# First product of the last stage on pairs of token blocks by seven block products, with its weights kept in DRAM

## The chip, the cores and the metric

One Trainium2 chip, one of its cores. The metric is device time in microseconds (us) of one execution; lower is better. Matrix work runs on TensorE (PE), element work on VectorE (DVE), ScalarE (ACT) and GpSimd (POOL); DMAs are issued by SyncE (SP) unless said otherwise. Each engine, SP included, takes its instructions strictly in the order in which they stand.

## The reference

All inputs are float32 values; the six weight matrices arrive as float64 words.

```python
# attention over keys and values averaged in groups of 8 (8 batches, 8 heads, 576 tokens, 64 features)
x = attention(q, k, v)                       # [4608, 512]
a = x @ w1; b = x @ w2                       # 512 -> 1024
x = (a * b @ w3) @ w_out                     # 1024 -> 1024 -> 512
h = x @ w_in2                                # 512 -> 2048, the first product of the last stage
g = h * (1.0 / (1.0 + np.exp(-1.702 * h)))
out = g @ w_out2                             # 2048 -> 512, the second product of the last stage
```

## The kernel before

The 4608 tokens are taken in 9 blocks of 512 (`T`). Every matrix operand is held as two float32r parts, hi (rounded to 12 bits) and lo (the rest), and a product is three matmuls, hi\*hi, hi\*lo and lo\*hi (`mm3`, L93 to L97), of 128x128 weights on 512 columns. `split` (L89) makes the pair: a cast on ACT (L90) and a subtraction on DVE or POOL (L91).

There are three stages. The first multiplies w3 by w_out, with the first attention beside it. The middle one walks over the 9 blocks (L502); a step `f` of its 8 steps multiplies x by 128 columns each of w1 and w2 into the banks wk0 and wk1 (24 matmuls), ACT copies the one, DVE multiplies it by the other (L518, written to `a`), the product is split (lo on POOL), and 12 matmuls of `x2_step` take it into the four banks acc. So a step is 36 matmuls. The bank wk1 is free for the next step only when DVE's L518 is done. `tick` puts the attention of later blocks between the steps. The block's result, x2, goes to DRAM (L489).

The last stage (L575) walks over the 9 blocks again, 16 steps `f` each: 12 matmuls of w_in2 on x2 (four groups of 128 features), a sigmoid on ACT (L584), a product on DVE (L585), a split with its lo on POOL, and two steps later 12 matmuls of `out_step` into acc. A step is 24 matmuls.

The float64 weights are converted by `Conv` (L108): a chunk of 128x512 words is loaded (512 KB), ACT makes two float32 pictures of its halves (L143, L144), DVE shifts and merges (L145, L148), POOL adds (L151), and a call `done` splits the result. `conv.step` has three chunks in work at a time; a `cv` tile has four buffers. The 32 chunks of w_in2 and w_out2 are queued behind block 7 of the middle stage (L534) and are converted, two a step, beside block 8 and the first block of the last stage, into SBUF tiles (`b_s1`, `b_s2`) that stay. Tiles of 4 KB a partition come from a list of 39 slots (`take`, `give`). The order in which instructions stand on each engine is settled by a scheduler that simulates a timeline; the program's order is its starting point.

## Time and profile before

| | |
|---|---|
| runs of the kernel | 1599.31, 1599.63, 1603.57 us; median 1599.63 |
| profiled execution, span from first to last instruction | 1599.4 us (its own run time is not listed apart) |
| mean granted clock of TensorE | 0.982 of 2.4 GHz |
| matmuls | 6760 |
| read from and written to HBM | 75.5 MB and 18.9 MB |
| middle stage, blocks 7 and 8 | about 657 to 800 us |
| last stage | about 800 to 1594 us |

The page gives busy time by engine, a row of tenths over the span, the chain of work that ended last, and groups of instructions by line. A window row gives, for a stretch, the busy time of each engine with its number of instructions, the granted clock (1.00 is 2.4 GHz, 0.50 is 1.2 GHz), and the share and rate of the DMA engines. In a timeline row, the time in brackets is how long the engine sat idle before, and what it waited for. Some matmul records can be missing.

### The profile page before, as it was taken

Reading aid. Unit: us, or ns where it says so; the run is one execution under the profiler, and the core shown is the slowest. Engines: PE = TensorE matmul, PEld = TensorE weight load, DVE = VectorE, ACT = ScalarE, POOL = GpSimd, SP = SyncE. Lnnn points to the kernel's source line nnn. Section 1 sums busy time; section 2 is a strip of 40 time slices with the busy share of each in tenths; the row PEclk is TensorE's granted clock in tenths of the full one; section 3 lists DMA queues with packets and bytes.
Section 4 is the critical chain, followed back from the end, with each engine's and each line's share of the span. In section 5 each row is a group of like instructions: output and inputs, shape, how many; then the busy total and the mean of one; then the engine's idle time right before and its main releaser. Section 6 shows DMA issues by size and latency. Waiting matters only on the chain.

```text
span 1599.4 us, 19097 instructions
## 1 busy us (share of the span) xinstructions
PE 1536.5 (96%) x6920; PEld 1267.0 (79%) x6920; DVE 756.8 (47%) x1458; ACT 587.2 (37%) x1130; POOL 714.2 (45%) x748
## 2 busy tenths in 40 slices
PE   5867999999999999999998999999999999999998
PEld 3645888888888888888786888888888888888887
...
GB/s 277 244 156 58 52 72 50 78 49 72 52 72 45 75 46 34 27 80 158 146 104 27 27 27 27 20 32 20 9 40 14 33 20 33 21 27 14 27 0 27
DMA packets 195488, 95.62 MB, mean 60 GB/s; under 512 B 155457, under 2 KB 171841, under 8 KB 195393
## 3 DMA queue, kind: packets, MB, share of 16 engines
...
q8 instruction: 54, 0.88, 0.2%
...
## 4 chain that ended last, share of the span: by engine, by line
PE 82%; DVE 8%; issue 3%; DMA 2%; ACT 2%; POOL 2%; SPq 1%; DVEq 0%; POOLq 0%; ACTq 0%
PE wk L95 15%; PE wk L96 15%; PE wk L97 15%; PE acc L97 11%; PE acc L96 11%; PE acc L95 11%; DVE cv L148 2%; PE wk L246 2%; DVE cv L145 2%; DVE s L91 2%; DMA s<-in_moe_w_out_dram 1%; DVE p L281 1%; DMA s<-in_moe_w_dram 1%; POOL s L91 1%; ACT s L90 1%
## 5 line engine op out<-in xcount | busy, mean ns | idle before, releaser
L95 PE MATMUL wk<-s,s 128*128 128x512 f32 x1152 | 453.5, 395 | 7.6 <-DVE a L518 4.3
L96 PE MATMUL wk<-s,s 128*128 128x512 f32 x1152 | 451.4, 392 | 2.0 <-DVE s L358 2.0
L97 PE MATMUL wk<-s,s 128*128 128x512 f32 x1152 | 450.8, 392 | 1.4 <-DVE s L91 1.4
L91 POOL TENSOR_TENSOR s<-sg,s 128x512 fp32r<-128x512 f32 x144 | 188.6, 1310 | 508.8 <-ACT s L90 508.8
L585 DVE TENSOR_TENSOR sg<-wk,sg 128x512 f32<-128x512 f32 x144 | 99.6, 692 | 619.5 <-ACT sg L584 619.5
L97 PE MATMUL acc<-s,s 128*128 128x512 f32 x928 | 363.7, 394 | 9.5 <-DVE s L91 5.1
L95 PE MATMUL acc<-s,s 128*128 128x512 f32 x928 | 364.7, 395 | 4.3 <-ACT s L90 4.3
L96 PE MATMUL acc<-s,s 128*128 128x512 f32 x928 | 364.4, 393 | 1.6 <-DVE s L91 1.1
L95 PEld LDWEIGHTS wk<-s,s 128*128 128x128 f32 x1152 | 217.7, 189 | 54.5 <-DVE a L518 5.6
L97 PEld LDWEIGHTS wk<-s,s 128*128 128x128 f32 x1152 | 217.9, 189 | 47.5 <-DVE s L91 1.8
L96 PEld LDWEIGHTS wk<-s,s 128*128 128x128 f32 x1152 | 217.8, 189 | 46.9 <-DVE s L358 2.4
L584 ACT ACTIVATE sg<-wk 128x512 f32<-128x512 f32 x144 | 86.1, 598 | 410.9 <-PE wk L97 410.8
L97 PEld LDWEIGHTS acc<-s,s 128*128 128x128 f32 x928 | 175.6, 189 | 48.6 <-DVE s L91 8.2
L95 PEld LDWEIGHTS acc<-s,s 128*128 128x128 f32 x928 | 175.4, 189 | 41.5 <-ACT s L90 7.2
L96 PEld LDWEIGHTS acc<-s,s 128*128 128x128 f32 x928 | 175.8, 189 | 38.1 <-POOL s L91 1.8
L91 POOL TENSOR_TENSOR s<-a,s 128x512 fp32r<-128x512 f32 x72 | 94.1, 1307 | 215.8 <-ACT s L90 174.9
L281 DVE STREAM_TRANSPOSE p<-s_t 32x160 f32<-32x160 f32 (+1 forms) x560 | 178.4, 319 | 10.8
L151 POOL TENSOR_TENSOR cv<-cv,s 128x512 int32<-128x512 int32 x72 | 105.4, 1465 | 71.9 <-DVE cv L148 52.1
L90 ACT CAST s<-sg 128x512 fp32r<-128x512 f32 x144 | 89.4, 621 | 112.0 <-DVE sg L585 111.0
L518 DVE TENSOR_TENSOR a<-wk,a 128x512 f32<-128x512 f32 x72 | 49.5, 687 | 78.1 <-PE wk L97 66.4
L148 DVE SCALAR_TENSOR_TENSOR cv<-s,cv 128x512 uint32<-128x512 uint32 x72 | 80.5, 1127 | 1.0
L145 DVE TENSOR_SCALAR cv<-cv 128x512 uint32<-128x512 uint32 x72 | 61.2, 857 | 30.9 <-ACT cv L143 30.7
...
## 6 DMA issues: line engine op xcount, KB each, us to landing
s<-in_moe_w_dram SPq DMA_DIRECT2D x32, 512.0 KB, 6.8
s<-in_moe_w_out_dram SPq DMA_DIRECT2D x24, 512.0 KB, 4.6
kr<-in_k_dram SPq DMA_DIRECT2D x128, 72.0 KB, 2.4
qr<-in_q_dram SPq DMA_DIRECT2D x128, 72.0 KB, 2.5
x2d<-x2o SPq DMA_DIRECT2D x36, 256.0 KB, 2.5
x2r<-x2d SPq DMA_DIRECT2D x36, 256.0 KB, 2.9
out_dram<-o SPq DMA_DIRECT2D x36, 256.0 KB, 2.0
vr<-in_v_dram SPq DMA_DIRECT2D x32, 256.0 KB, 2.7
```

What stands on the lines that cost most here:

```text
L90: nc.scalar.copy(dst[:, 0], src)
L91: lo_eng.tensor_tensor(out=dst[:, 1], in0=src, in1=f32(dst[:, 0]), op=ALU.subtract)
L95: nc.tensor.matmul(o, a[:, 0, a_sl], b[:, 0, b_sl], start=first, stop=False)
L96: nc.tensor.matmul(o, a[:, 0, a_sl], b[:, 1, b_sl], start=False, stop=False)
L97: nc.tensor.matmul(o, a[:, 1, a_sl], b[:, 0, b_sl], start=False, stop=last)
L145: nc.vector.tensor_scalar(out=wu, in0=wu, scalar1=4, scalar2=1, op0=ALU.logical_shift_left, op1=ALU.logical_shift_right)
L148: nc.vector.scalar_tensor_tensor(out=wu, in0=hi_w, scalar=0x80000000, in1=wu, op0=ALU.bitwise_and, op1=ALU.bitwise_or)
L151: nc.gpsimd.tensor_tensor(out=w.bitcast(I32), in0=w.bitcast(I32), in1=lo_w.bitcast(I32), op=ALU.add)
L281: nc.vector.transpose(out=dst[:, :nt, 32 * c:32 * c + 32], in_=s_t[32 * c:32 * c + 32, :nt, 32 * r:32 * r + 32])
L518: nc.vector.tensor_tensor(out=a, in0=pb_, in1=a, op=ALU.mult)
L584: nc.scalar.activation(a, ps, AF.Sigmoid, scale=1.702)
L585: nc.vector.tensor_tensor(out=a, in0=ps, in1=a, op=ALU.mult)
```

## The change

**The first product of the last stage.** Blocks 1 to 8 are taken in four pairs. For a pair, the operand w_in2 is cut in two halves of its 512 inputs and two halves of its 2048 outputs, and x2 in two halves of its features and the pair's two blocks. The 2x2 block product is made with seven products instead of eight (`ORDER`: M1 to M7, each two 128-deep `mm3`, so 6 matmuls, into one of three banks), and the sums between them are made on DVE, partly while a bank is still being accumulated (`tt` after M6, `q` after M7). A step `f` of a pair stands for two output groups (f and f+8) of both blocks; it has 42 matmuls of the first product, and beside it stand 24 matmuls of the second product for the pair's first block. The second block's gated values wait in `g2`; when the 8 steps are over, they are split and multiplied in 16 `out_step`s of 12 matmuls, with `x_prep` of the next pair beside them: seven combinations of x2, each in two halves (on DVE 14 subtractions of `split` and 8 that form the combinations, from 8 loads of x2). Block 0 is taken alone as before.

**The weights.** Seven weight blocks are needed for each `f`: A11, A12, A22, and sums S1 to S4; block 0 needs A21 too. `units` and `win_second` make them from two converted chunks and write them to DRAM as hi/lo pairs (`win_d`, 2 MB for each of 8 `f`); w_out2 goes to DRAM the same way (`wout_d`). The last stage loads w_out2 once, and streams `win_d` through five buffers `st`, for block 0 and again for each pair (`pull`).

**When they are converted.** The 32 chunks are queued ahead of block 7 of the middle stage, not behind it, and all are finished before the last stage: first the 16 chunks of w_in2, then the 16 of w_out2. A pool `pc` takes the place of the attention's `pa` there and gives 9 more slots.

**The rest.** The last stage has pools of its own for SBUF and PSUM; in block 0 the conversion is gone; the output tile `o` has two buffers instead of four; the middle stage's last x2 is stored by ACT's queue. The instruction counts move thus: PE 6760 matmuls to 6568, DVE 1459 to 1797 instructions, ACT 1129 to 1205, POOL 750 to 676, SP 501 to 705.

```diff
+    win_d = [dr_p.tile([P, 8, 2, HU], F32, name=f"wind{f}", tag=f"wind{f}") for f in range(NP1)]
+    wout_d = [dr_p.tile([P, 2, T], F32, name=f"woutd{f}", tag=f"woutd{f}") for f in range(NF2)]
...
+    def resplit(t, lo_eng):
...
+        nc.scalar.copy(t[:, 0], f32(t[:, 1]))
+        lo_eng.tensor_tensor(out=t[:, 1], in0=f32(t[:, 1]), in1=f32(t[:, 0]), op=ALU.subtract)
...
+        def units(f, u0, u1, w, eng):
...
+            t = take((P, 2, 2, HU))
+            v = w.rearrange("p (u m) -> p u m", u=2)
+            nc.scalar.copy(t[:, :, 0], v)
+            eng.tensor_tensor(out=t[:, :, 1], in0=v, in1=f32(t[:, :, 0]), op=ALU.subtract)
+            nc.sync.dma_start(win_d[f][:, u0:u1 + 1], f32(t))
+            give(t)
...
+        def win_first(f):
+            def done(w):
+                hold[0] = w
+                units(f, A11, A12, w, nc.vector)
+            return done
+        def win_second(f):
+            def done(w):
+                h = hold[0]
+                a11, a12 = h[:, :HU], h[:, HU:]
+                a21, a22 = w[:, :HU], w[:, HU:]
+                units(f, A21, A22, w, nc.gpsimd)
+                c = take((P, 2, T), F32)
+                cs = c.rearrange("p a (b m) -> p (a b) m", b=2)
+                for o, p0_, p1_, op, eng in (
+                        (0, a21, a22, ALU.add, nc.vector), (2, a11, a21, ALU.subtract, nc.gpsimd),
+                        (1, cs[:, 0], a11, ALU.subtract, nc.vector),
+                        (3, a12, cs[:, 1], ALU.subtract, nc.gpsimd)):
+                    eng.tensor_tensor(out=cs[:, o], in0=p0_, in1=p1_, op=op)
+                units(f, S1, S2, c[:, 0], nc.vector)
+                units(f, S3, S4, c[:, 1], nc.gpsimd)
+                give(c)
+            return done
...
+                    (nc.scalar if blk == NB - 1 else nc.sync).dma_start(x2_d[blk][:, m], st)
...
+            if blk == NB - 2:
...
+                free[:0] = [(pa, NSLOT + i) for i in range(NX)]
+                for f in range(NP1):
+                    conv.add(col_tile(w_in2, f), None, win_first(f))
+                    conv.add(col_tile(w_in2, f + NP1), None, win_second(f))
+                for f in range(NF2):
+                    conv.add(row_tile(w_out2, f), None, wout_done(f))
+                conv.depth, conv.keep = 5, 5
+                conv.load()
...
-            if blk == NB - 2:
-                for f in range(NF2):
-                    conv.add(col_tile(w_in2, f), None, conv.to(b_s1, f))
-                    conv.add(row_tile(w_out2, f), None, conv.to(b_s2, f, nc.vector))
-                conv.load()
-            if blk < NB - 1:
-                give(*(xs.pop((blk, c)) for c in range(KM)))
+            give(*(xs.pop((blk, c)) for c in range(KM)))
...
-        rest, conv.todo = conv.todo, []
-        while any(conv.line):
-            st, conv.staged = conv.staged, []
+        while conv.busy():
             conv.step()
...
+        def pull():
...
+            if todo:
+                key, src = todo.pop(0)
+                i = st_n[0] % NST
+                st_n[0] += 1
+                t = pb.tile([P, 2, 2, HU], F32R, name="st", tag=f"st{i}")
+                nc.sync.dma_start(f32(t[:, :src.shape[1]]), src)
+                ready[key] = t
...
+        def mm3u(o, w, j, b, first, last):
+            m = sl(j)
+            for n, (x, y) in enumerate(((0, 0), (0, 1), (1, 0))):
+                nc.tensor.matmul(o, w[:, x, m], b[:, y], start=first and n == 0,
+                                 stop=last and n == 2, skip_group_check=True)
...
+        ORDER = (("M1", A11, 0, True), ("M6", S2, 1, True), ("M5", S1, 2, True), ("M7", S3, 1, False),
+                 ("M2", A12, 0, False), ("M4", A22, 1, False), ("M3", S4, 2, False))
+        HS = {A11: (0, 0), A12: (0, 1), S1: (1, 0), S2: (1, 1), S3: (2, 0), S4: (2, 1), A22: (3, 0)}
...
+        def x_prep(pr):
...
+            def load(jj):
+                for n, (c, b) in enumerate(((jj, b0), (jj, b0 + 1), (2 + jj, b0), (2 + jj, b0 + 1))):
+                    raw[jj, n] = tmp(("m1", "m1", "tt", "q")[n], 2 if n < 2 else 1)
+                    nc.sync.dma_start(raw[jj, n], x2_d[b][:, c])
...
+        for _ in range(3):
+            pull()
...
+        for c in range(KM):
+            t = gtile(c, F32R)
+            nc.sync.dma_start(f32(t[:, 1]), x2_d[0][:, c])
+            resplit(t, nc.vector if c % 2 else nc.gpsimd)
+            x.append(t)
...
+        for f in range(NF2):
+            bk = bank()
+            w = ready.pop(("h", 0, f, 0))
+            for c in range(KM):
+                mm3u(bk[1], w[:, c // 2], c % 2, x[c], c == 0, c == KM - 1)
+            pull()
...
+            if len(pend) > 2:
+                out_step(outs)
+            if f >= 4:
+                prep.pop(0)()
...
+        for pr in range(1, NPAIR + 1):
+            X = xc.pop(pr)
+            outs = [bank() for _ in range(4)]
+            g2 = []
+            for f in range(NP1):
...
+                ga, gb = moving(), moving()
+                g2.append(gtile(f))
+                c12, c22 = g2[f][:, 0], g2[f][:, 1]
...
+                def gate(v, eng):
+                    sg = tmp("sg", 2)
+                    nc.scalar.activation(sg, v, AF.Sigmoid, scale=1.702)
+                    eng.tensor_tensor(out=v, in0=v, in1=sg, op=ALU.mult)
+                for name, u, b, first in ORDER:
+                    o = B[b][1]
+                    s, h = HS[u]
+                    w = ready["h", pr, f, s]
+                    for j in range(2):
+                        mm3u(o, w[:, h], j, X[name, j], first and j == 0, j == 1)
+                    if name == "M1":
+                        m1 = tmp("m1", 2)
+                        nc.scalar.copy(m1, o)
+                    elif name == "M6":
+                        tt = tmp("tt", 1)
+                        nc.vector.tensor_tensor(out=tt, in0=o, in1=m1, op=ALU.add)
+                    elif name == "M7":
+                        q_ = tmp("q", 1)
+                        nc.vector.tensor_tensor(out=q_, in0=o, in1=m1, op=ALU.add)
+                        nc.vector.tensor_tensor(out=c22, in0=B[2][1], in1=q_, op=ALU.add)
+                        gate(c22, nc.gpsimd)
+                        pull()
+                    elif name == "M2":
+                        sg = tmp("sg", 2)
+                        nc.scalar.activation(sg, o, AF.Sigmoid, scale=1.702)
+                        nc.vector.tensor_tensor(out=sg, in0=o, in1=sg, op=ALU.mult)
+                        freed(B[0])
+                        split(ga, sg, nc.vector)
+                        pull()
+                    elif name == "M4":
+                        c21 = tmp("o", 2)
+                        nc.vector.tensor_tensor(out=c21, in0=o, in1=m1, op=ALU.add)
+                        freed(B[1])
+                        gate(c21, nc.vector)
+                        split(gb, c21, nc.vector)
+                        pull()
+                    elif name == "M3":
+                        nc.vector.tensor_tensor(out=c12, in0=o, in1=tt, op=ALU.add)
+                        freed(B[2])
+                        gate(c12, nc.gpsimd)
+                        pull()
...
+                while pend:
+                    out_step(outs)
+                pend.append((f, ga, f == 0, False))
+                pend.append((f + NP1, gb, False, f == NP1 - 1))
...
+            prep = x_prep(pr + 1) if pr < NPAIR else []
+            order = [(f, h) for f in range(NP1) for h in range(2)]
+            n, outs2 = 0, None
+            while pend:
+                while n < NF2 and len(pend) < NMV:
+                    f, h = order[n]
+                    g = moving()
+                    split(g, g2[f][:, h], nc.vector)
+                    pend.append((f + h * NP1, g, n == 0, n == NF2 - 1))
+                    n += 1
+                if prep:
+                    prep.pop(0)()
+                if pend[0][2]:
+                    store(outs, 2 * pr - 1)
+                    outs2 = [bank() for _ in range(4)]
+                out_step(outs2 or outs)
```

Three places show how the instructions stand. The names: `cv` is a chunk in conversion, `a` the middle stage's product, `s` a slot, `m_`, `tt`, `q`, `o`, `sg` single float32 tiles, `g_` the second block's gated values, `mv` a split operand of the second product, `bk_` a bank, `xM_` a split combination of x2, `wind_` and `woutd_` the weights in DRAM.

First, DVE in the middle stage, between two products `a`. Before, in block 8, where chunks of w_in2 and w_out2 take turns:

```order
L518 TENSOR_TENSOR a<-wk_68,a 128x512 [waits PE_49]
L145 TENSOR_SCALAR cv<-cv 128x512 [waits Activation_49]
L148 SCALAR_TENSOR_TENSOR cv<-s_6693,cv 128x512 [waits DMAHW2_49,DVE_49]
L91 TENSOR_TENSOR s_6973<-cv,s_6973 128x512 [waits Activation_49]
L145 TENSOR_SCALAR cv<-cv 128x512 [waits Activation_49]
L148 SCALAR_TENSOR_TENSOR cv<-s_6769,cv 128x512 [waits DVE_49]
L145 TENSOR_SCALAR cv<-cv 128x512 [waits Activation_49]
L518 TENSOR_TENSOR a<-wk_68,a 128x512 [waits PE_49]
```

Now, in block 7, where the chunks of w_in2 are made:

```order
L574 TENSOR_TENSOR a<-wk_68,a 128x512 [waits PE_49]
L420 TENSOR_TENSOR s_6782<-cv,s_6782 128x2x256 [waits Activation_49]
L156 TENSOR_SCALAR cv<-cv 128x512 [waits Activation_49,Pool_49]
L444 TENSOR_TENSOR s_6840<-cv 128x256 [waits Pool_49]
L159 SCALAR_TENSOR_TENSOR cv<-s_6628,cv 128x512 [waits DVE_49]
L444 TENSOR_TENSOR s_6840<-s_6840,cv 128x256 [waits DVE_49]
L420 TENSOR_TENSOR s_6845<-s_6840,s_6845 128x2x256 [waits DMAHW4_49,Activation_49]
L420 TENSOR_TENSOR s_6861<-cv,s_6861 128x2x256 [waits Activation_49]
L444 TENSOR_TENSOR s_6919<-cv 128x256 [waits Pool_49]
L574 TENSOR_TENSOR a<-wk_68,a 128x512 [waits PE_49,Activation_49]
```

Between two products there stood six conversion instructions, and now eight: the subtractions of `units` (L420) and the sums of weight blocks (L444, 256 columns) have come in.

Second, PE and DVE in a pair's first product. Before, a step's 12 matmuls of the first product waited for one bank and DVE made one product a step (L585). PE now, from the end of M7 of one `f` (bank bk_8709) over the second product and M1 of the next `f` to M4, which goes on in M7's bank:

```order
L644 MATMUL bk_8709<-xM_8145,st 128x512 x3
L108 MATMUL bk_8199<-wo_7931,mv 128x512
L106 MATMUL bk_8200<-wo_7931,mv 128x512
L107 MATMUL bk_8200<-wo_7931,mv 128x512
L108 MATMUL bk_8200<-wo_7931,mv 128x512
L106 MATMUL bk_8201<-wo_7931,mv 128x512
L107 MATMUL bk_8201<-wo_7931,mv 128x512
L108 MATMUL bk_8201<-wo_7931,mv 128x512
L644 MATMUL bk_8814<-xM_7758,st 128x512 [waits DMAHW3_49]
L644 MATMUL bk_8814<-xM_7758,st 128x512 x2
L644 MATMUL bk_8814<-xM_8071,st 128x512 x3
L644 MATMUL bk_8709<-xM_7990,st 128x512 [waits DMAHW4_49,DVE_49]
```

DVE now, one whole step of a pair and the head of the next:

```order
L798 TENSOR_TENSOR tt<-bk_9895,m_9906 128x512 [waits PE_49]
L801 TENSOR_TENSOR q<-bk_9895,m_9906 128x512 [waits PE_49]
L802 TENSOR_TENSOR g_9899<-bk_9896,q 128x512 [waits DVE_49]
L808 TENSOR_TENSOR sg<-bk_9894,sg 128x512 [waits Activation_49]
L814 TENSOR_TENSOR o<-bk_9895,m_9906 128x512 [waits PE_49]
L97 TENSOR_TENSOR mv<-sg,mv 128x512 [waits Activation_49]
L820 TENSOR_TENSOR g_9899<-bk_9896,tt 128x512 [waits PE_49]
L785 TENSOR_TENSOR o<-o,sg 128x512 [waits Activation_49]
L97 TENSOR_TENSOR mv<-o,mv 128x512 [waits Activation_49]
L798 TENSOR_TENSOR tt<-bk_10001,m_10012 128x512 [waits PE_49]
```

M4 waits for DVE (`q` has to be read out first); 13 matmuls stand between M7 and M4. DVE has nine instructions a step; the first product of the same two output groups and two blocks had four (L585) before, and its four splits took POOL.

Third, SP at the hand-over between the stages. Before, conversion chunks and x2 are loaded in turn and nothing in the list stores a weight. Now:

```order
L454 DMA woutd_93<-s_7513 128x1024 [waits DMAHW5_49,DVE_49]
L454 DMA woutd_92<-s_7473 128x1024 [waits DMAHW6_49,Pool_49]
L454 DMA woutd_94<-s_7517 128x1024 [waits DMAHW7_49,Pool_49]
L624 DMA st<-wind_71 128x1024 [waits DMAHW4_49,PE_49]
L624 DMA st<-wind_72 128x1024 [waits DMAHW5_49]
L624 DMA st<-wind_73 128x1024 [waits DMAHW6_49,PE_49]
L737 DMA g_7537<-x2d_95 128x512 [waits DMAHW7_49]
L737 DMA g_7541<-x2d_95 128x512 [waits DMAHW0_49,PE_49,Pool_49]
L737 DMA g_7545<-x2d_95 128x512 [waits DMAHW1_49]
L737 DMA g_7549<-x2d_95 128x512 [waits DMAHW2_49]
```

The last stage's first loads (`st`, then x2 of block 0 into `g_`) stand behind the last stores of w_out2, which wait for POOL.

## Rows read from the trace of the kernel before

**Rows 1.** The page, part 1: busy us (share of span) and instructions by engine.
```profile
PE 1536.5 (96%) x6920; PEld 1267.0 (79%) x6920; DVE 756.8 (47%) x1458; ACT 587.2 (37%) x1130; POOL 714.2 (45%) x748
```

**Rows 2.** Windows: busy us (instructions) PE, PEld, DVE, ACT, POOL; clock, DMA share, GB/s.
```profile
870.00:1500.00 630.00, 630.00 (x2781) 521.81 (x2781) 90.12 (x131) 167.34 (x275) 187.19 (x145) 1.00 0.08 24
```

**Rows 3.** Timeline, PE, steady last stage: start us, length us, engine, line, operation.
```profile
1202.35 0.39 PE L95 MATMUL wk<-s,s 128*128 128x512 f32 x1
...
1205.07 0.39 PE L95 MATMUL acc<-s,s 128*128 128x512 f32 x1
```

**Rows 4.** Windows again, where the last stage's weights are converted.
```profile
750.00:780.00 30.00, 25.70 (x112) 20.24 (x110) 24.24 (x25) 17.11 (x31) 25.70 (x18) 1.00 0.29 90
780.00:790.00 10.00, 10.00 (x37) 8.10 (x38) 5.09 (x5) 6.17 (x11) 6.54 (x6) 0.83 0.75 248
840.00:870.00 30.00, 24.41 (x90) 18.67 (x89) 19.95 (x20) 14.28 (x26) 26.99 (x20) 0.89 0.07 20
```

**Rows 5.** Timeline, POOL, while the weights are converted.
```profile
757.23 1.47 POOL L91 TENSOR_TENSOR s<-cv,s 128x512 fp32r<-128x512 f32 x1
...
773.50 1.75 POOL L91 TENSOR_TENSOR s<-x2r,s 128x512 fp32r<-128x512 f32 x1
...
831.84 1.29 POOL L91 TENSOR_TENSOR s<-cv,s 128x512 fp32r<-128x512 f32 x1
```

**Rows 6.** Timeline, DVE, over the same stretch and the step before it.
```profile
663.55 0.69 DVE L518 TENSOR_TENSOR a<-wk,a 128x512 f32<-128x512 f32 x1 [6.80 <-PE wk L97]
671.71 0.69 DVE L518 TENSOR_TENSOR a<-wk,a 128x512 f32<-128x512 f32 x1 [7.47 <-PE wk L97]
...
748.83 0.68 DVE L518 TENSOR_TENSOR a<-wk,a 128x512 f32<-128x512 f32 x1
...
769.65 0.68 DVE L148 SCALAR_TENSOR_TENSOR cv<-s,cv 128x512 uint32<-128x512 uint32 x1
...
774.01 1.78 DVE L91 TENSOR_TENSOR s<-cv,s 128x512 fp32r<-128x512 f32 x1
...
778.86 0.41 DVE L145 TENSOR_SCALAR cv<-cv 128x512 uint32<-128x512 uint32 x1
779.20 0.68 DVE L518 TENSOR_TENSOR a<-wk,a 128x512 f32<-128x512 f32 x1
```

**Rows 7.** Windows: the three steps from 748.83 to 779.20 alone.
```profile
748.83:779.20 30.37, 26.80 (x116) 21.14 (x114) 24.61 (x26) 17.92 (x31) 26.07 (x18) 1.00 0.28 87
```

**Rows 8.** Groups by form, DVE, of those three steps: count, busy us, mean ns.
```profile
L148 DVE SCALAR_TENSOR_TENSOR cv<-s,cv 128x512 uint32<-128x512 uint32 x8 | 11.9, 1487 | 0.2
L145 DVE TENSOR_SCALAR cv<-cv 128x512 uint32<-128x512 uint32 x9 | 7.6, 839 | 5.6 <-ACT cv L143 5.6
L91 DVE TENSOR_TENSOR s<-cv,s 128x512 fp32r<-128x512 f32 x5 | 5.6, 1117 | 0.0
```

**Rows 9.** Groups by form, whole span: count, busy us, mean ns, idle before.
```profile
L291 POOL TENSOR_TENSOR va<-vr 128x256 f32<-128x256 f32 x32 | 24.0, 749 | 0.0
L585 DVE TENSOR_TENSOR sg<-wk,sg 128x512 f32<-128x512 f32 x144 | 99.6, 692 | 619.5 <-ACT sg L584 619.5
L584 ACT ACTIVATE sg<-wk 128x512 f32<-128x512 f32 x144 | 86.1, 598 | 410.9 <-PE wk L97 410.8
```

**Rows 10.** DMA issues of the page: count, KB each, median us to landing.
```profile
s<-in_moe_w_out_dram SPq DMA_DIRECT2D x24, 512.0 KB, 4.6
out_dram<-o SPq DMA_DIRECT2D x36, 256.0 KB, 2.0
```

**Rows 11.** The tile view of w_out2's loads: landing times of its 512 KB DMAs.
```profile
DMA to landing us min/median/max: 3.3/4.6/11.3
```

**Rows 12.** Windows: four microseconds in which many loads run.
```profile
808.00:812.00 4.00, 4.00 (x19) 3.34 (x18) 4.00 (x4) 1.84 (x4) 3.93 (x3) 1.00 1.08 384
```

**Rows 13.** Timeline, DVE and SP, the end of the span.
```profile
1593.77 1.29 DVE L572 COPY o<-acc 128x512 f32<-128x512 f32 x2 [6.32 <-PE acc L97]
1594.16 1.79 SPq L573 DMA_DIRECT2D out_dram<-o  x4
```

More of the change, by code (lines that the diff above doesn't have):

```diff
@@ L63, in pooled_attention_moe_moe2 @@
     ESC = 1.0 / (D ** 0.5) / POOL
-    slot_p = ctx.enter_context(tc.tile_pool(name="slot", bufs=1))
-    ps_p = ctx.enter_context(tc.tile_pool(name="ps", bufs=1, space=PSUM))
+    slot_ctx, ps_ctx, pa_ctx = ExitStack(), ExitStack(), ExitStack()
+    slot_p = slot_ctx.enter_context(tc.tile_pool(name="slot", bufs=1))
+    ps_p = ps_ctx.enter_context(tc.tile_pool(name="ps", bufs=1, space=PSUM))
     dr_p = ctx.enter_context(tc.tile_pool(name="dr", bufs=1, space=DRAM))
-    NSLOT = 39
+    NSLOT, NX = 39, 9
     free = [(slot_p, i) for i in range(NSLOT)]
     held = {}
-    acc = [ps_p.tile([P, T], F32, name=f"acc{i}", tag=f"acc{i}") for i in range(4)]
-    wk = [ps_p.tile([P, T], F32, name=f"wk{i}", tag=f"wk{i}") for i in range(4)]
+    acc = [ps_p.tile([P, T], F32, name=f"acc{i}", tag=f"bank{i}") for i in range(4)]
+    wk = [ps_p.tile([P, T], F32, name=f"wk{i}", tag=f"bank{i + 4}") for i in range(4)]
+    HU = 2 * P
+    NP1 = NF2 // 2
+    A11, A12, S1, S2, S3, S4, A21, A22 = range(8)
+    win_d = [dr_p.tile([P, 8, 2, HU], F32, name=f"wind{f}", tag=f"wind{f}") for f in range(NP1)]
+    wout_d = [dr_p.tile([P, 2, T], F32, name=f"woutd{f}", tag=f"woutd{f}") for f in range(NF2)]
     x2_d = [dr_p.tile([P, KM, T], F32, name=f"x2d{b}", tag=f"x2d{b}") for b in range(NB)]
@@ L167, in pooled_attention_moe_moe2 @@
     cv_p = [None]
-    with tc.tile_pool(name="pa", bufs=1) as pa:
+    with pa_ctx:
+        pa = pa_ctx.enter_context(tc.tile_pool(name="pa", bufs=1))
         cv_p[0] = pa
@@ L394, in tick, with wout_done, done @@
                 g_vb(n)
-        wo_s, wp_s, w1_s, w2_s, b_s1, b_s2 = {}, {}, {}, {}, {}, {}
+        wo_s, wp_s, w1_s, w2_s = {}, {}, {}, {}
         NIT = DF1 // P
         w3_s = {}
+        def units(f, u0, u1, w, eng):
[5 more added lines that the diff above has]
+            give(t)
+        hold = [None]
+        def win_first(f):
[20 more added lines that the diff above has]
+            return done
+        def wout_done(f):
+            def done(w):
+                t = take()
+                split(t, w, nc.gpsimd if f % 2 else nc.vector)
+                nc.sync.dma_start(wout_d[f], f32(t))
+                give(t)
+            return done
         def w3_turn(it, jh):
@@ L488, in x2_step @@
                         nc.vector.tensor_copy(st, acc[m])
[L489 to L500 removed]
+                    (nc.scalar if blk == NB - 1 else nc.sync).dma_start(x2_d[blk][:, m], st)
         for blk in range(NB):
             x = [x_slot(blk, c) for c in range(KM)]
+            if blk == NB - 2:
+                pa_ctx.close()
+                pa = pa_ctx.enter_context(tc.tile_pool(name="pc", bufs=1, reuse_waits="tile"))
+                cv_p[0] = pa
+                free[:0] = [(pa, NSLOT + i) for i in range(NX)]
[6 more added lines that the diff above has]
+                conv.load()
             for f in range(NF1):
```

174 lines of the change are left out of this document (108 added, 66 removed).

## The prediction

> **What bounds the kernel now.** I read the page's engine line first: PE is busy for 96% of the span, the next engine, DVE, for 47% [rows 1]. So the matmuls set the time, and the question for each stretch is whether PE runs without gaps and at full clock. From 870 to 1500 us it does: 630.0 of 630 us busy, clock 1.00 (2.4 GHz) [rows 2]. There twelve matmuls take 1205.07 − 1202.35 = 2.72 us [rows 3], 0.2267 us each. A step of the middle stage without conversion takes 671.71 − 663.55 = 8.16 us from one `a` to the next [rows 6], which is 36 matmuls at that price.
>
> Next I looked for stretches that fall short. They lie where w_in2 and w_out2 are converted: PE idles 4.30 us from 750 to 780 and 5.59 us from 840 to 870; from 780 to 790 the clock is 0.83 (part of it at 1.2 GHz), which costs 10 × 0.17 = 1.7 us, and from 840 to 870 it is 0.89, 3.3 us [rows 4]. Together 15 us that conversion costs now.
>
> Why conversion holds PE up stands in rows of DVE and POOL. A DVE instruction with two operands in SBUF takes 0.68 us alone and 1.78 us beside POOL; the shift of L145 takes 0.41 us alone [rows 6]. POOL's subtraction takes 1.29 us alone, 1.47 in company of L145, and 1.75 in company of a DVE instruction with two SBUF operands [rows 5]: 0.18 and 0.45 us more. Three converting steps, from `a` at 748.83 to `a` at 779.20 [rows 6], took 30.37 us instead of 3 × 8.16 = 24.5; POOL had 18 instructions there [rows 7], DVE 8 of L148, 9 of L145 and 5 of L91 [rows 8]. 18 × 1.29 + 13 × 0.45 + 9 × 0.18 = 30.7 us, which is the time measured. So there POOL, lengthened by DVE, sets the step. PE waits because wk1 comes free only with DVE's `a`, which stands behind the conversion instructions.
>
> **The change, part by part.** Each sum is made against the profiled span of 1599.4 us, 0.2 us under the median of the runs, so the result needs no shift.
>
> *Matmuls.* 6760 become 6568: 48 fewer a pair, 192 in all. At 0.2267 us that is **−43.5 us**, if PE stays as full as it is now.
>
> *Old conversion.* Its 15 us vanish from block 8 and the first block of the last stage: **−15 us**.
>
> *New conversion, block 7.* A step now makes both chunks of one `f` of w_in2. POOL has per step two adds (L162), two subtractions of `units` (L420) and the split of `a`, five at 1.29 us, and two of 256 columns, 0.75 us by the nearest row [rows 9]: 8.0 us. DVE beside it has two L156 (0.18 each), two L159 and two L420 (0.45 each), and two L444 of half the width (some 0.25): 2.7 us. That makes 10.6 us a step against 8.16, so 8 × 2.45 = **+20 us**. From below, POOL alone fits into 8.16, and nothing is lost; from above, the full lengths of the DVE instructions add, 33 us (worked out with the second rival). I take 20, since the formula is the one that gave 30.7 for 30.4.
> Here the Trainium skill speaks against the change. By "SBUF — State Buffer", section "SBUF: two separate sides", a DVE instruction with two SBUF inputs and a GpSimd instruction exclude each other for a whole instruction, and the loser blocks fully, so that whole durations add. By it the term would be those 33 us. The measured three steps disagree: 23.2 us of POOL and 12.5 us of DVE at its lone lengths would make 35.7 us, and they took 30.4.
>
> *New conversion, block 8.* For two chunks of w_out2 POOL has two adds, one split and the split of `a`, 4 × 1.29 = 5.2 us, lengthened by DVE's two L156, two L159 and one split, 1.7 us: 6.9 us, under 8.16. **0**, from 0 to 8.
> The stores are new on SP's queue: 25.2 MB of loads and stores of w_in2's blocks within some 85 us is 296 GB/s, under the 384 GB/s that a stretch of loads shows [rows 12]. The cover is thin, but slots and `cv` buffers let transfers wait a step. ACT's casts lie beside DVE's work.
>
> *Hand-over.* SP issues the last stage's first loads behind the last store of w_out2, which waits for POOL. Then come three `st` and the x2 tiles, some 1.75 MB. At 384 GB/s that is 4.6 us, then a cast (0.60, like the activation [rows 9]) and POOL's 1.29 us; the last split and eight matmuls cover about 3. With the store's wait I take **+6 us**, from 0 to 12 (the longest 512 KB load took 11.3 us [rows 11]).
>
> *Block 0.* Its converted weights now come from DRAM instead of being made here: 12.6 MB at 384 GB/s take 33 us, while PE works through it in 16 steps of 24 matmuls, 87 us; each load is due in order. **0**, up to 5.
>
> *Pairs, first product.* A step is 66 matmuls, 14.96 us. DVE's nine instructions at 0.69 us (L585's [rows 9]) take 6.2 us, ACT's seven at 0.60 take 4.2, POOL's two products 2.6: all covered twice over. What counts is order. M7's bank is read by `q` while 13 matmuls (2.95 us) pass before M4 writes into it; `q` needs about 0.8. The stream of `win_d` is 14.7 MB in a pair's first 117 us, 126 GB/s; a 512 KB load lands in 3.3 us at best, 4.6 in the median, 11.3 at worst [rows 11], and a buffer is reused with some 54 matmuls (12 us) in hand, at a pair's start with 26 to 29 (6 us). If two loads a pair landed late by 11.3 − 5.9 = 5.4 us, it would cost 43 us; with the median nothing. The larger loads of w_out2 have a median of 4.6 us too [rows 10], and these come in a quieter stretch, so I go with the median.
>
> *Pairs, second product.* 16 × 2.72 = 43.5 us of PE, with some 40 DVE instructions of 0.69 us, 27.6 us, among them 14 splits and 8 sums of the next pair. No wait, unless the first split of the next pair is late. For all five changes of phase, and for the pairs, I take **+3 us**, from 0 to 12.
>
> *Clock.* Where PE was idle for part of a stretch, the granted clock fell to 0.83 and 0.89 of full [rows 4], but stayed at 1.00 from 750 to 780 with 25.70 of 30 us busy. Block 7 will have PE busy for 8.16 of 10.6 us, less than either. **+3 us**, two spells like that of 780 to 790; from 0 to 14 (0.83 through all 85 us of block 7).
>
> *End.* A store of `out` takes 2.0 us [rows 10]. With two tiles the last copy waits for the store before the last: the fourth copy starts when the second's store has landed, about 1 us behind where it now starts, at the last matmul's end [rows 13]. **+1 us**, from 0 to 1.5.
>
> Sum: 1599.4 − 43.5 − 15 + 20 + 0 + 6 + 0 + 3 + 3 + 1 = **1573.9 us**. Forecast 1574. With block 7 between 10 and 30, and the rest as it falls, its own range is 1562 to 1586.
>
> **The rivals.**
> - *Conversion hides.* The scheduler lets blocks 7 and 8 share the load: both together need 8 × (10.6 + 6.9) = 140 us of POOL against 131 us of PE, and POOL's instructions alone fit. Then block 7 costs about nothing: 1554. For it: 39 plus 9 slots let chunks wait. Against it: DVE's order shows eight conversion instructions ahead of `a`, as for a step that does a whole `f`. 0.23.
> - *Whole durations add.* If in block 7 each DVE instruction with two SBUF operands and each L156 blocks POOL for its full length, a step takes 8.0 + 4 × 0.68 + 2 × 0.36 + 2 × 0.41 = 12.3 us: 33 us in place of 20, 1587. Against it: the 30.4 us above. 0.11. This is the rule of the page named before.
> - *The clock falls* to 0.83 through block 7: 14 us in place of 3, 1585. For it: PE is less busy there than in either stretch that lost clock. 0.04.
> - *M4 waits for `q`*, the side on which it gets slower. If two DVE instructions of 1.7 us stand ahead of `q` when M7 ends, M4 starts 3.4 + 0.8 − 2.95 = 1.25 us late, in each of 32 steps: 40 us, 1614. It decides from the point at which `q` starts more than 2.15 us behind M7. Against it: in DVE's order only `tt` stands directly ahead, and M6 ends 25 matmuls (5.7 us) before M7. For it: DVE has twice the work that it had, beside POOL's products. 0.07.
>
> That the change doesn't do what it says is excluded by the instruction list, with its 192 fewer matmuls.
>
> **How the numbers follow.** Forecast 0.55, the rivals 0.23, 0.11, 0.04 and 0.07. What can be told from no change is 0.3%, 4.8 us: under 1594.8 is faster, over 1604.4 slower. The forecast gives 0.53 to faster and 0.02 to same, the first rival 0.23 to faster, the second 0.09 and 0.02, the third 0.03 and 0.01, the last 0.07 to slower: 0.88, 0.05, 0.07. The range runs from 1550, under the first rival, to 1594, which holds the second and third with some 7 us more of loads that land late; outside it are the last rival and the ends.
>
> **What would show it.** In the changed kernel: 6568 matmuls; in block 7 products `a` (L574) 10.6 us apart (8.2 if the first rival holds, 12.3 with the second), with L159 and L420 near 1.7 us on DVE; in block 8 8.2 us apart; a gap of some 6 us at the hand-over; each pair 8 × 14.96 + 43.5 = 163 us with PE idle near 0; clock 1.00 from block 0 on. I am wrong if PE idles within the pairs, on DVE's `q` or `tt` or on a load of `st`, or if block 8 is held up too.

## The result, and the profile after

The changed kernel took 1579.26 us (median of 4 runs, 1577.45 to 1580.45), the kernel before 1600.12 in the same comparison: a ratio of 0.9868, 95% interval 0.9854 to 0.9882, 1.3% faster. The forecast was 1574, its own range 1562 to 1586. The profiled execution has a span of 1575.7 us (1577.45 with what lies around it).

The page's engine line, beside [rows 1]: 192 matmuls fewer (6920 to 6728 with the transposes), PE busy 36 us less, DVE 251 us more.

```profile
PE 1500.1 (95%) x6728; PEld 1233.7 (78%) x6728; DVE 1007.7 (64%) x1796; ACT 619.2 (39%) x1202; POOL 617.0 (39%) x674
```

Windows of the changed kernel (columns as in [rows 2]): the end of block 7 and the start of block 8, most of the rest of block 8, its end with the hand-over and block 0, and then the pairs.

```profile
700.00:760.00 60.00, 49.72 (x205) 38.80 (x205) 55.36 (x53) 31.54 (x57) 55.38 (x40) 0.97 0.90 320
760.00:800.00 40.00, 39.85 (x176) 32.55 (x175) 32.47 (x33) 23.80 (x42) 29.73 (x21) 1.00 0.68 268
800.00:880.00 80.00, 66.43 (x257) 51.98 (x256) 34.80 (x43) 28.35 (x47) 26.97 (x20) 0.87 0.79 289
880.00:1570.00 690.00, 690.00 (x3045) 571.12 (x3043) 304.78 (x441) 208.03 (x359) 91.14 (x70) 1.00 0.34 108
```

Block 8 is not over at 800 us: its last matmul ends at 815.6. From the last product `a` of block 6 to that of block 7, on to this matmul, both together, and from it to 880 us:

```profile
653.91:734.17 80.26, 72.58 (x317) 58.60 (x316) 65.36 (x68) 42.71 (x77) 61.68 (x46) 1.00 0.75 263
734.17:815.62 81.45, 74.20 (x304) 58.74 (x303) 63.37 (x63) 43.95 (x77) 63.58 (x44) 0.94 0.74 279
653.91:815.62 161.71, 146.77 (x620) 117.33 (x618) 128.73 (x129) 86.66 (x154) 125.26 (x89) 0.97 0.74 271
815.62:880.00 64.38, 55.31 (x221) 44.33 (x222) 26.62 (x35) 23.64 (x39) 16.33 (x12) 0.89 0.84 307
```

From 880 us on PE is full at 1.00, as in [rows 2]: the pairs lose nothing. All that is lost lies from 700 to 880: 10.3 + 0.2 + 13.6 = 24 us of idle PE, and by the clock at most 60 × 0.03 + 80 × 0.13 = 12 us. What PE waited for in that time, from 640 to 900 us (who waited, on what; us in all, times, longest):

```profile
PE wk L106 <- DVE a L574: 7.3, 5, 2.6
PE bk L644 <- ACT g L101: 7.0, 2, 5.6
PE acc L106 <- ACT s L96: 4.0, 1, 4.0
PE wk L106 <- ACT a L573: 3.2, 2, 1.9
PE bk L644 <- DMA st<-wind: 2.1, 1, 2.1
```

In block 7 the products `a` settle at (734.17 − 690.69) / 4 = 10.9 us apart; the last two steps of block 8 are far longer than 8.16 (DVE's timeline):

```profile
690.69 0.68 DVE L574 TENSOR_TENSOR a<-wk,a 128x512 f32<-128x512 f32 x1
...
734.17 0.68 DVE L574 TENSOR_TENSOR a<-wk,a 128x512 f32<-128x512 f32 x1
...
783.33 0.68 DVE L574 TENSOR_TENSOR a<-wk,a 128x512 f32<-128x512 f32 x1
...
796.08 0.68 DVE L574 TENSOR_TENSOR a<-wk,a 128x512 f32<-128x512 f32 x1
...
806.87 0.68 DVE L574 TENSOR_TENSOR a<-wk,a 128x512 f32<-128x512 f32 x1
```

The conversion instructions are stretched as in [rows 8]: groups of the changed kernel, 660 to 830 us, mean ns of one behind the busy time.

```profile
L159 DVE SCALAR_TENSOR_TENSOR cv<-s,cv 128x512 uint32<-128x512 uint32 x31 | 38.0, 1231 | 0.7
L156 DVE TENSOR_SCALAR cv<-cv 128x512 uint32<-128x512 uint32 x31 | 32.1, 1041 | 11.2 <-ACT cv L154 7.0 <-DMA s<-in_moe_w_in_dram 3.9
L162 POOL TENSOR_TENSOR cv<-cv,s 128x512 int32<-128x512 int32 x31 | 47.7, 1542 | 17.4 <-DVE cv L159 10.3 <-DMA s<-in_moe_w_in_dram 3.7 <-issue 2.2
```

The hand-over in PE's timeline, with idle time in brackets:

```profile
809.31 2.07 PE L106 MATMUL acc<-s,s 128*128 128x512 f32 x4 [4.05 <-ACT s L96]
...
821.23 2.56 PE L644 MATMUL bk<-g,st 128*128 128x512 f32 x5 [5.62 <-ACT g L101]
...
825.19 13.71 PE L644 MATMUL bk<-g,st 128*128 128x512 f32 x51 [1.39 <-ACT g L101]
...
855.47 4.81 PE L644 MATMUL bk<-g,st 128*128 128x512 f32 x13 [2.06 <-DMA st<-wind]
```

The 5.62 us end with the cast of the first x2 tile. SP issues its load only behind the last stores of w_out2 and three `st` loads, and it lands after 7.0 us; the three other loads of x2 go out at 820.69 (SP's and ACT's timelines):

```profile
809.34 1.56 SPq L454 DMA_DIRECT2D woutd<-s  x2
810.99 1.76 SPq L624 DMA_DIRECT2D st<-wind  x3
813.58 0.32 SPq L737 DMA_DIRECT2D g<-x2d  x1
...
820.69 1.57 SPq L737 DMA_DIRECT2D g<-x2d  x3
```

```profile
820.56 0.62 ACT L101 CAST g<-g 128x512 fp32r<-128x512 f32 x1 [5.12 <-DMA g<-x2d]
```

The idle stretch is followed by one at a granted clock of 0.50, 1.2 GHz (windows):

```profile
816.00:820.00 4.00, 0.00 (x0) 0.00 (x0) 0.42 (x1) 0.00 (x0) 0.00 (x0) 0.87 1.01 355
820.00:824.00 4.00, 2.56 (x5) 1.33 (x5) 0.00 (x0) 0.62 (x1) 1.27 (x1) 0.50 0.87 267
824.00:828.00 4.00, 2.81 (x7) 2.23 (x8) 1.31 (x2) 2.49 (x4) 1.15 (x1) 0.50 0.93 290
```

### The profile page after: what moved, and what is told of

Its sections match the earlier page's. It is cut to its first block, busy times and chain, and to the rows that moved or that the text cites. A ratio compares the mean times of both kernels' runs of the same rounds, so it can differ in the third digit from the quotient of the medians.

```text
span 1575.7 us, 19586 instructions
## 1 busy us (share of the span) xinstructions
PE 1500.1 (95%) x6728; PEld 1233.7 (78%) x6728; DVE 1007.7 (64%) x1796; ACT 619.2 (39%) x1202; POOL 617.0 (39%) x674
## 4 chain that ended last, share of the span: by engine, by line
PE 81%; DVE 8%; DMA 4%; issue 3%; POOL 1%; SPq 1%; ACT 1%; DVEq 0%; POOLq 0%; ACTq 0%
PE bk L644 22%; PE bk L108 8%; PE bk L107 8%; PE bk L106 8%; PE wk L108 7%; PE wk L106 7%; PE wk L107 7%; PE acc L108 3%; PE acc L107 3%; PE acc L106 3%; DVE cv L156 2%; PE wk L258 2%; DVE cv L159 2%; DMA s<-in_moe_w_dram 1%; DVE s L97 1%
## 5 line engine op out<-in xcount | busy, mean ns | idle before, releaser
L644 PE MATMUL bk<-xM,st 128*128 128x512 f32 x1344 | 319.1, 389 | 0.0
L644 PEld LDWEIGHTS bk<-xM,st 128*128 128x128 f32 x1344 | 252.3, 188 | 52.7 <-ACT o L661 0.4
L785 POOL TENSOR_TENSOR g<-g,sg 128x512 f32<-128x512 f32 x64 | 83.4, 1303 | 529.3 <-ACT sg L784 529.3
L106 PE MATMUL wk<-s,s 128*128 128x512 f32 x576 | 228.9, 399 | 15.0 <-DVE a L574 8.3
L107 PE MATMUL wk<-s,s 128*128 128x512 f32 x576 | 226.8, 394 | 2.0 <-DVE s L370 2.0
L108 PE MATMUL wk<-s,s 128*128 128x512 f32 x576 | 226.4, 394 | 1.4 <-DVE s L97 1.4
L107 PE MATMUL bk<-wo,mv 128*128 128x512 f32 x576 | 224.1, 389 | 0.0
L106 PE MATMUL bk<-wo,mv 128*128 128x512 f32 x576 | 223.9, 389 | 0.0
L108 PE MATMUL bk<-wo,mv 128*128 128x512 f32 x576 | 208.8, 389 | 0.0
L293 DVE STREAM_TRANSPOSE p<-s_t 32x160 f32<-32x160 f32 (+1 forms) x560 | 178.4, 319 | 10.8
L106 PE MATMUL acc<-s,s 128*128 128x512 f32 x352 | 141.4, 407 | 7.1 <-ACT s L96 7.1
L108 PE MATMUL acc<-s,s 128*128 128x512 f32 x352 | 141.8, 403 | 5.1 <-DVE s L97 5.1
L107 PE MATMUL acc<-s,s 128*128 128x512 f32 x352 | 141.0, 400 | 0.9 <-POOL s L97 0.7
L106 PEld LDWEIGHTS wk<-s,s 128*128 128x128 f32 x576 | 108.8, 189 | 40.8 <-DVE a L574 10.6
L108 PEld LDWEIGHTS wk<-s,s 128*128 128x128 f32 x576 | 109.4, 190 | 24.8 <-DVE s L97 1.8
L107 PEld LDWEIGHTS wk<-s,s 128*128 128x128 f32 x576 | 109.5, 190 | 24.3 <-DVE s L370 2.4
L784 ACT ACTIVATE sg<-g 128x512 f32<-128x512 f32 x64 | 40.5, 633 | 217.0 <-DVE g L802 198.0
L107 PEld LDWEIGHTS bk<-wo,mv 128*128 128x128 f32 x576 | 108.1, 188 | 22.5
L106 PEld LDWEIGHTS bk<-wo,mv 128*128 128x128 f32 x576 | 108.1, 188 | 22.4
L108 PEld LDWEIGHTS bk<-wo,mv 128*128 128x128 f32 x576 | 108.1, 188 | 22.4
L162 POOL TENSOR_TENSOR cv<-cv,s 128x512 int32<-128x512 int32 x72 | 105.3, 1465 | 49.1 <-DVE cv L159 27.3
```

What stands on the lines that cost most here:

```text
L106: nc.tensor.matmul(o, a[:, 0, a_sl], b[:, 0, b_sl], start=first, stop=False)
L107: nc.tensor.matmul(o, a[:, 0, a_sl], b[:, 1, b_sl], start=False, stop=False)
L108: nc.tensor.matmul(o, a[:, 1, a_sl], b[:, 0, b_sl], start=False, stop=last)
L162: nc.gpsimd.tensor_tensor(out=w.bitcast(I32), in0=w.bitcast(I32), in1=lo_w.bitcast(I32), op=ALU.add)
L293: nc.vector.transpose(out=dst[:, :nt, 32 * c:32 * c + 32], in_=s_t[32 * c:32 * c + 32, :nt, 32 * r:32 * r + 32])
L644: nc.tensor.matmul(o, w[:, x, m], b[:, y], start=first and n == 0, stop=last and n == 2, skip_group_check=True)
```

## The experiments

My theory after the result: conversion and what it leaves over for the hand-over cost all of the 24 + 12 = 36 us, and the seven products nothing. Rivals: the products or their loads cost time too; the DMA engines, not DVE and POOL, pace the conversion.

**What the two conversions cost.** The kernel before, its late chunks plainly loaded:

```diff
-                    conv.add(col_tile(w_in2, f), None, conv.to(b_s1, f))
-                    conv.add(row_tile(w_out2, f), None, conv.to(b_s2, f, nc.vector))
+                    conv.todo += [(b_s1, f), (b_s2, f)]
...
+                t = take()
+                nc.sync.dma_start(f32(t), x2_d[0][:, :2])
```

> The kernel before, with the engine work of the 32 late chunks left out: each chunk is a plain 512 KB load of x2 values into the slot that the last stage reads (its output is not the reference's). By the prediction's term of 15 us for the old conversion: 1600 - 15 = 1585 us (1583 to 1588). Rival (the old conversion cost less, PE's idle time there was made up elsewhere): over 1590. The difference to the changed kernel without conversion should be the 192 matmuls, 43.5 us less 1 for the tail; if it is under 38, the seven products cost something themselves.

1584.15 us (1600.87 for the kernel before), 16.7 less. PE has no gap in this window:

```profile
640.00:880.00 240.00, 240.00 (x1064) 198.91 (x1063) 33.30 (x57) 54.68 (x92) 57.64 (x45) 1.00 0.29 90
```

So the 15 us were there, and 1584.15 − 43.5 = 1541 is what the seven products would reach with no loss. The changed kernel without conversion:

```diff
-                for f in range(NP1):
-                    conv.add(col_tile(w_in2, f), None, win_first(f))
-                    conv.add(col_tile(w_in2, f + NP1), None, win_second(f))
-                for f in range(NF2):
-                    conv.add(row_tile(w_out2, f), None, wout_done(f))
...
+                    dst, src = fill.pop(0)
+                    nc.sync.dma_start(dst, f32(src))
```

> The changed kernel without any conversion of w_in2 and w_out2: their 32 chunks are neither loaded, converted nor stored; in blocks 1 to 6 the DRAM tiles win_d and wout_d are filled with tiles of w3*w_out, so the last stage streams the same bytes (its output is not the reference's). Theory (all that the changed kernel loses to PE lies in the conversion and what follows it, and the pairs lose nothing): the changed kernel's PE idles 24 us and its clock costs some 11 us between 690 and 860 us, so 1579 - 35 = 1544 us (1541 to 1549). Rival (loads of x2, st and w_out2 at the hand-over cost time by themselves): some 8 us stay there, 1552. Rival (the seven products lose time in the pairs): over 1555, with PE idle after the hand-over.

1575.56 us, which says nothing: the added stores read tiles that are ready early, the scheduler probably moved them ahead of the attention's loads, and PE stood there for two long waits:

```profile
PE wk L359 <- ACT vm L317: 24.8, 1, 24.8
PE wk L359 <- ACT pt L350: 9.5, 1, 9.5
```

With a source that is ready only in its own block (`x[2 * (f % 2) + c]`):

> As e1_no_conv, but the DRAM tiles are filled in blocks 1 to 6 with x of the block in work, so that the fill cannot be moved ahead of the first attention's loads, where it held PE up (25 and 10 us of waits in the first 300 us). In e1_no_conv the last product a of block 6 came at 678.4 us, in the changed kernel at 653.9; less these 24.5 us its span was 1549, that is 27 under the changed kernel's 1575.7. So 1552 us (1549 to 1556) if conversion costs 27 and the hand-over by itself 8 to 9; 1544 if the hand-over costs nothing without conversion.

1554.91 us: conversion costs 24 us, not 36. The other 14 us over 1541 stay without it, as the rival on the hand-over's loads had it (8 us there): windows place most at the hand-over, with 4.1 us idle behind 800 us and 2.3 just ahead, where PE already waits for x2 of block 0, and up to 4.8 by the clock; the last `a` of block 6 came 2.7 us later than in the changed kernel (656.57 against 653.91). The two kernels without conversion lie 29.2 us apart, less than the 38 under which the products themselves were to be suspected. But from 860 to 1540 us PE is busy throughout, so the rival that the pairs cost something falls.

```profile
700.00:800.00 100.00, 97.70 (x429) 80.36 (x428) 10.37 (x15) 16.15 (x27) 16.62 (x13) 1.00 0.12 41
800.00:880.00 80.00, 75.95 (x319) 61.67 (x319) 28.77 (x38) 27.87 (x46) 20.27 (x15) 0.94 0.68 245
656.57:796.25 139.68, 139.68 (x620) 115.48 (x618) 16.19 (x25) 23.70 (x42) 21.93 (x17) 1.00 0.09 29
```

The last row runs, as 653.91 to 815.62 does in the changed kernel, from the last `a` of block 6 to the last matmul of block 8: the same 620 matmuls, without a gap in 139.7 us. So conversion costs 161.7 − 139.7 = 22 us in blocks 7 and 8, 14.9 of them idle and 7.1 more busy time (mean clock 0.97).

**Engines or DMA.** The stores left out:

```diff
-            nc.sync.dma_start(win_d[f][:, u0:u1 + 1], f32(t))
...
-                nc.sync.dma_start(wout_d[f], f32(t))
```

> The changed kernel with all conversion work on the engines, but without the stores of win_d and wout_d (25 MB); the DRAM tiles are filled in blocks 1 to 6 with tiles of w3*w_out (its output is not the reference's). Theory (engines set the pace of the conversion, POOL with DVE): blocks 7 and 8 stay as they are, products a some 10.6 us apart in block 7; only waits on landed stores go, 0 to 8 us: 1571 to 1579. Rival (the DMA engines, over 0.9 busy from 704 to 780 and from 816 to 860 us, set it): conversion ends earlier, the gap at the hand-over closes: 1550 to 1562.

> As e3_no_stores, with the fill of e1b. Less the 23 us that the fill cost there, that run was at 1580, 5 us over the changed kernel. Theory (engines set the conversion's pace): 1577 to 1586. Rival (DMA sets it): 1562 or less.

The first took 1606.99 us with the fill's waits in it, the second 1584.44: 5 us more than the changed kernel, not 17 less. From 700 to 800 us the DMA engines are busy for 0.35 of the time instead of 0.81, and PE idles 18.2 us instead of 10.4. So the DMA engines don't pace the conversion. The sums left out (with the first fill, which cost 23 us ahead of block 7 here):

```diff
-                units(f, S1, S2, c[:, 0], nc.vector)
-                units(f, S3, S4, c[:, 1], nc.gpsimd)
```

> The changed kernel without the sums S1 to S4 and without A21 and A22's... no: A11, A12, A21, A22 are split and stored, the sums S1 to S4 are neither formed, split nor stored; their DRAM tiles hold tiles of w3*w_out from blocks 1 to 6 (the output is not the reference's). POOL has 5.2 us a step in block 7 instead of 8.0, DVE four instructions fewer, stores of w_in2 half. Theory (POOL lengthened by DVE sets block 7's step): 5.2 + 1.7 = 6.9 us, under 8.16, products a 8.2 us apart; the 12 us lost in blocks 7 and 8 go and the conversion ends some 15 us earlier, so the hand-over loses little: 1550 to 1556. Rival (DMA): with 8.4 MB less to store a part of it, 1560 to 1570.

1595.65 us. Its span, 1591.6, less those 23 is 1568: a gain of 7, not of 23 to 29. (The number lies in the DMA rival's range, but the run without stores excludes that rival.) The freed time did not go to PE: from 704.0 to 735.2 us POOL made eleven adds (L162), 3.1 us apart, where the changed kernel needs 10.9 us for two, and DVE is as full as there (36.63 of 40 us). It looks as if chunks were converted as early as buffers allow, however many fall into one step. The window, 700 to 740 us:

```profile
700.00:740.00 40.00, 37.13 (x160) 29.40 (x159) 36.63 (x35) 22.83 (x40) 31.14 (x21) 1.00 0.72 249
```

**Moving and pacing the work.** The chunks of w_out2 in blocks 1 to 6 (with this, w_in2's are taken three in two steps in blocks 7 and 8, not two a step):

```diff
+            if 1 <= blk < NB - 2:
+                for f in range(3 * blk - 3, min(3 * blk, NF2)):
+                    conv.add(row_tile(w_out2, f), None, wout_done(f))
+                conv.depth, conv.keep = 1, 3
...
-                if conv.busy():
+                if conv.busy() and (blk < NB - 2 or f % 2 == 0):
```

> The changed kernel with the 16 chunks of w_out2 converted in blocks 1 to 6, three a block, and stored to DRAM there; the 16 chunks of w_in2 stay queued ahead of block 7. Theory (conversion of two chunks a step costs 2.4 us a step in block 7, and the rest of the loss is the work of w_out2 that is left over at the end of block 8): block 7 as in the changed kernel, products a 10.6 us apart; block 8 from its second third and the hand-over lose only the 9 us that stay without conversion: 1579 - 14 = 1565 us (1560 to 1570). Rival (DVE, 80% busy with attention in blocks 1 to 6, has no room): PE waits there, over 1575.

1567.85 us, as expected, 11 less. Block 7 takes 81.2 us from `a` to `a`, against 80.3 in the changed kernel, so the gain lies behind it: it is what w_out2's chunks cost at the end of block 8 and at the hand-over. Then w_in2's chunks one a step, each loaded into the slot that the step's second product gave back:

```diff
+                if blk >= NB - 2:
+                    free.insert(0, free.pop())
+                    conv.depth = len(conv.staged) + 1
+                    conv.load()
+                    conv.depth = 0
```

> e4_wout_early, and the chunks of w_in2 are paced: after each step's second product one chunk is loaded into the slot which that product has just given back, and one is converted a step, so that the 16 spread over blocks 7 and 8. POOL then has some 6 us a step of 8.16. Theory: products a 8.2 us apart in both blocks, PE full there; only the hand-over loses 9 us: 1553 us (1549 to 1558). Rival (the loads, now in series with the products, make `a` or the split wait): as e4_wout_early, 1565.

1565.69 us, a miss: 2 us less than the run before, within its scatter, where 15 were expected. The products came 6.1 to 10.5 us apart, and PE still idles 5.5 us in these windows, against 10.4 in the changed kernel; 3.4 of them it waits for ACT's copy that frees the other bank, wk0. What holds that copy up no run tells apart. The kernel also reached the end of block 6 some 5 us later than the changed kernel (658.99 against 653.91).

```profile
700.00:760.00 60.00, 55.04 (x235) 43.27 (x234) 28.90 (x36) 24.65 (x43) 35.20 (x28) 1.00 0.54 185
760.00:800.00 40.00, 39.47 (x171) 31.92 (x172) 16.97 (x23) 14.71 (x25) 22.84 (x19) 1.00 0.54 193
```

```profile
PE wk L106 <- ACT a L576: 3.4, 5, 1.0
```

**The hand-over.** Are the loads late because their tiles lie in slots that are given back last? The tiles in another order, alone and on top of each of the two above; each of the three has its own order, and this is the head of one:

```diff
+        for tag in ("g0 wo4 x x sg wo7 x wo12 g1 wo2 wo15 g2 wo14 wo8 x g3 ...").split():
...
+                t = pb.tile([P, 2, T], F32R, name=tag, tag=tag)
...
+            pre[tag] = t
```

> The changed kernel with the placing alone; w_out2's chunks are converted at the end of block 8 as in it. Theory (at its hand-over SP stands at the last stores of w_out2, which wait for POOL until 811 us, so early slots do not help): 1576 to 1581, as the changed kernel, with the first x2 load still issued behind 810 us. Rival (the slots alone made the 5.6 us gap): 1570 to 1573.

> e7_paced with the last stage's tiles placed so that the first `st`, x2 of block 0, sigmoid and split tiles lie where the middle stage's slots are given back early; nothing else changes. In e7_paced the hand-over still lost some 10 us (x2 of block 0 waited for slots that the last products hold; then 9 loads of w_out2 stood ahead of an `st` load). Theory: the stores of win_d end before block 8 does, so the loads of `st` and x2 now land before PE is done with block 8: 1565.7 - 8 = 1558 us (1555 to 1561). Rival (loads are late because SP issues them behind the last stores and the DMA engines are full, the place of the tiles does not matter): 1563 to 1567.

> e4_wout_early with the same placing of the last stage's tiles; w_in2's chunks are not paced. Here SP has no conversion left for most of block 8, so by the theory its loads come well ahead: 1567.9 less 8 = 1560 us (1557 to 1563). If it is as fast as e8_paced_placed or faster, pacing is worth nothing.

1580.02, 1565.12 and 1568.40 us: the place is worth nothing in any of the three. The second and third were misses, 4 and 5 us above their ranges. The profile of the second gave away what holds x2's loads up; the row for the changed kernel (SP's waits, 640 to 860 us: sum, times, longest) says the same:

```profile
SPq L737 <- DMA x2d<-x2o: 7.0, 2, 6.7
```

SP waits for the last stores of x2 before it may issue the second to fourth load of x2 of block 0, a block stored long ago. (The first load does not wait for them.) In the changed kernel's instruction lists, ACT's stores (first two rows) and SP's loads name the same completion semaphores:

```
L545 DMA x2d_103<-x2o 128x512 [waits DMAHW0_49,Activation_49]
L545 DMA x2d_103<-x2o 128x512 [waits DMAHW1_49,DVE_49]
L737 DMA g_7541<-x2d_95 128x512 [waits DMAHW0_49,PE_49,Pool_49]
L737 DMA g_7545<-x2d_95 128x512 [waits DMAHW1_49]
```

The stores can go only when PE is done with block 8. So:

```diff
-                    (nc.scalar if blk == NB - 1 else nc.sync).dma_start(x2_d[blk][:, m], st)
+                    (nc.gpsimd if blk == NB - 1 else nc.sync).dma_start(x2_d[blk][:, m], st)
...
-            resplit(t, nc.vector if c % 2 else nc.gpsimd)
+            resplit(t, nc.vector)
```

> e8_paced_placed with the four stores of block 8's x2 issued by POOL's queue instead of ACT's, and the lo parts of block 0's x2 all made on DVE. In e8 and in the changed kernel SP waits 9.3 and 7.0 us for these stores before it may issue the second to fourth load of block 0's x2: the instruction lists show loads and stores that name the same completion semaphores (DMAHW0 to DMAHW2), and the stores, ACT's, can only go when PE is done with block 8. In this kernel's list POOL's stores name none of them. Theory (this shared semaphore makes the gap at the hand-over): SP issues these loads without that wait by 801 us, loads of w_out2 and st follow some 10 us earlier; PE waits 1.9 us once at the hand-over instead of 3.7 in all, not at all for st (3.8 us in e8), and the spells at 1.2 GHz go: 1565.1 - 8 = 1557 us (1554 to 1561). Rival (the loads are late because the DMA engines are full): 1563 to 1567, with the same waits.

1560.05 us, 5 less (4 by the ratios to the kernel before, 0.9753 against 0.9778), and the fastest of the runs that do the whole work; the ratio's interval is 0.9737 to 0.9768. SP's timeline without and with the edit, the four loads of x2 in one row, then PE's waits from 790 to 900 us, and the window from block 8's last matmul to 880 us, each first without:

```profile
798.66 10.64 SPq L768 DMA_DIRECT2D g<-x2d  x4
```

```profile
799.27 2.45 SPq L768 DMA_DIRECT2D g<-x2d  x4
```

```profile
PE bk L657 <- DMA st<-wind: 3.8, 1, 3.8
PE bk L657 <- ACT g L101: 3.3, 2, 1.9
```

```profile
PE bk L657 <- DMA st<-wind: 3.7, 1, 3.7
PE bk L657 <- ACT g L101: 0.8, 1, 0.8
```

```profile
805.62:880.00 74.38, 66.86 (x274) 54.03 (x274) 26.74 (x37) 26.35 (x44) 19.39 (x14) 0.93 0.74 265
```

```profile
807.03:880.00 72.97, 68.45 (x287) 55.73 (x288) 27.74 (x40) 27.27 (x46) 18.36 (x17) 0.95 0.71 266
```

The loads go out in 2.5 us instead of 10.6, all of them by 801.7, and the stores start only at 806.6: so the loads needed neither data nor a buffer of the stores, and the shared semaphore made SP's wait. Of PE's 3.3 us 0.8 is left, and with 13 matmuls more in 1.4 us less the stretch gains some 4 us. How much of that belongs to the semaphore is not told apart: ACT's queue no longer issues the four stores just ahead of its casts, and a wait of 0.4 us for POOL's lo part is gone too. The wait for `st` was to go and stays at 3.7, so there the rival may hold: SP still issues nine loads of w_out2 ahead of that load. Nor are the spells of low clock gone (0.95 in the last row).

## Why the prediction was right, point by point

- *Matmuls, −43.5*: right. 1584.15 − 1554.91 is 29.2 between the kernels without conversion; with what the second loses at its hand-over (6.4 idle, up to 5 by the clock) and its 2.7 us ahead of block 7 that makes up to 43.
- *Old conversion, −15*: right, 16.7.
- *Block 7, +20*: the step was right (10.9 us against 10.6), the count was not. The first three steps took 25.6 us together, hardly more than without conversion, since only three chunks reached POOL in them (its L162); five steps ran at 10.9. PE idles 7.7 us from 653.91 to block 7's last `a`. The rule of whole durations (the Trainium skill, "SBUF — State Buffer", section "SBUF: two separate sides") would make 12.3 us of a step; the measured 10.9 is nearer to the sum of partial lengths. That the two engines hold each other up, as the Trainium skill says there, is in the trace: L156 takes 1.04 us in the mean and 0.41 alone, POOL's add 1.54, where a POOL instruction alone takes 1.29. But both engines are nearly full from 700 to 740 us (DVE 37.5 of 40 us, POOL 38.0), and without the sums DVE alone is, so that POOL sets the step, as the term has it, is not shown.
- *Block 8, 0*: failed. "For two chunks of w_out2 ... 6.9 us, under 8.16" took two chunks a step for granted. w_out2's chunks began late, behind w_in2's, and the last steps took 12.75 and 10.8 us with four and three (DVE's L159). PE idles 7.3 us up to block 8's last matmul, 4.0 of them for the split of the last `a`: that product came only at 806.87, behind three chunks on DVE, and its cast behind another one on ACT.
- *Hand-over, +6, and block 0, 0*: the mechanism was right, the size short. PE idles 9.1 us behind block 8's last matmul: 5.6 for the first load of x2, which stands behind w_out2's last stores as forecast and lands in 7.0 us among other transfers; 1.4 for loads of x2 that wait for the stores of block 8's x2, which I had not seen; 2.1 for `st` in block 0.
- *Clock, +3*: mis-sized, it cost up to 12: 7.1 us more busy time for the same matmuls in blocks 7 and 8, and behind them 55.3 us of busy time for 221 matmuls that take 50.1 at 0.2267. The term counted two spells and none behind the hand-over's gap. It also misread its row: from 780 to 790 us PE was busy all the time [rows 4], and its idle time lay before.
- *Pairs, +3*: 0. `q` was never late, and no load of `st` after 880 us. *End, +1*: 0.2, from PE's last matmul to the end of the span.

So the forecast had 15 us too much (block 7 and the pairs) and 20 too little (block 8, hand-over, clock). The cause was right, conversion that holds PE up where it is made and at the change of stage; that the sum came out within 5 us was luck. Of the rivals none decided: the conversion did not hide (10.9 us a step), durations did not add in full, the clock was 0.97 or more in every step of block 7, and M4 did not wait.
